# A recurrence feeding a routed expert layer on one core: outputs and evacuations first in the planner's queues, longer assumed waits

## The chip, the cores and the metric

The kernel runs on one core of a Trainium2 chip. The metric is device time of one execution in microseconds (us). The engines are TensorE (PE; its weight loads are shown as PEld), VectorE (DVE), ScalarE (ACT), GpSimd (POOL) and SyncE (SP, which only issues DMAs here).

## What is computed

Two layers follow one another. The first is a gated linear recurrence over the sequence, for 4 batches of 5056 steps and 256 channels; the second sends each of the 20224 rows to one of 8 experts, chosen by cosine similarity.

```python
sig = 1.0 / (1.0 + np.exp(-f_logit))
f = lower_bound + (1.0 - lower_bound) * sig
for t in range(S):
    h = f[:, t] * h + (1.0 - f[:, t]) * x[:, t]
    y[:, t] = h
x = y.reshape(B * S, D)                      # 20224 x 256
logits = xn @ en.T / tau                     # both normalised by row
expert_idx = np.argmax(logits, axis=1)
gate_w = softmax(logits)[rows, expert_idx]
for e in range(8):
    h = np.maximum(x[mask] @ w1[e], 0.0)     # 256 -> 1024
    out[mask] = gate_w[mask, None] * (h @ w2[e])   # 1024 -> 256
```

## The kernel before

**Recurrence.** The rows are cut into 40 chunks of 512 (the last has 256). For a chunk, `F_` and `X_` transpose the loaded gate logits and inputs on TensorE (lines 546 and 575), ScalarE makes the gate (554, 560), VectorE the product and the scan (583, 599). `Y_` transposes the result back (618) and ScalarE copies it into a row buffer (626). Two chunks are a group; `route_` computes logits, the best expert and each row's slot, and `gate_` the gate weight, which begins with a power function on POOL (775). `gate_` serves two groups at once (four chunks), except at the end, where it serves one group.

**Scratch.** Then POOL scatters these rows, 128 at a time, into a scratch tensor in HBM that is sorted by expert (line 832): 16 indirect DMAs for four chunks, which I call a set. A row carries its gate weight and its original row number.

**Experts.** `update_` counts rows for each expert and writes a table of complete tiles of 256 rows. It runs after the groups listed in line 1107; the last one covers all rows and fills the last tiles up with null rows. There are 86 tiles. `tile_` loads one with SyncE (996), and that load waits for every scratch scatter up to its update's group. TensorE transposes it (1013), VectorE copies that (1021), TensorE multiplies with the first weights in four steps (1036), ScalarE and VectorE take two each of the four results out of PSUM with a ReLU (1051, 1056), TensorE multiplies with the second weights (1067), ScalarE and VectorE evacuate one half each with the gate weight (1081, 1085), and POOL scatters the halves to their original rows (1091). There are 6 buffers of loaded tiles, 4 of outputs. For the first 70 tiles the first product has two PSUM banks and the second one, since the recurrence needs the others; after that four and two.

**Order.** Each engine works through a fixed list, in order, and waits for semaphores on the way. The lists come from a planner that runs when the program is built (`schedule`): it gives each operation an assumed cost, lets a dependent on another engine start `LAT` ns after its producer's end, and models a DMA as `DMA_FIX` ns behind a common bus of `DMA_RATE` bytes per ns. Where more than one operation of an engine is ready in the plan, the one with the lowest `prio` goes first. Recurrence, routing, gate and scratch scatters have the number of their chunk as `prio` (for a set, that of its last chunk). The operations of a tile have a number by these lines, in which `avail` lists the update that makes each tile complete; a tile's transposes and copy have 1.5 less:

```python
k = max(0, -(-(tok - E * (T - 1)) // T)) if u < len(ups) - 1 else NT
avail += [(u, g)] * (k - len(avail))
...
pr.prio = groups[g][-1] + 3.0 + 0.5 * (j - avail.index((u, g)))
```

Of the kernel before, what the change touches and what calls it, by code (L numbers as in the profile page):

```python
# [16 lines left out]
class Op:  # L17
    __slots__ = (
        "eng", "fn", "deps", "order", "dma", "val", "know", "used", "cost", "nbytes", "prio",
        "idx", "start", "end", "tag",  # L20
    )


class Prog:
# [2 lines left out]

    LAT = 90  # L30
    DMA_FIX = 1900
    DMA_RATE = 300.0

    def __init__(self):
        self.ops = []
# [55 lines left out]
    def schedule(self):  # L91
# [19 lines left out]
        while True:  # L111
# [22 lines left out]
            if o.dma is not None:  # L134
                bus = max(bus, free[e]) + o.nbytes / self.DMA_RATE
                o.end = max(bus, free[e]) + self.DMA_FIX
# [3 lines left out]
            for q, hard in succ[id(o)]:  # L140
                t = (o.end + self.LAT) if hard else free[e]
                if q.eng == e and o.dma is None and hard:
# [75 lines left out]
def bass_hgrn_recurrence__then__cosine_router_kernel(  # L218
# [22 lines left out]
    RW = 264  # L241
# [11 lines left out]
    pr = Prog()  # L253
    op = pr.op

    with ExitStack() as es:

        def sb(name, shape, dt=F32):
            return es.enter_context(nc.sbuf_tensor(name, shape, dt))
# [39 lines left out]
        Yt = [sb(f"Yt{q}", [P, 16, RW], BF16) for q in range(NY)]  # L299
# [28 lines left out]
        xsb = [sb(f"xsb{q}", [P, 2, RW], BF16) for q in range(NX)]  # L328
        ys = [sb(f"ys{q}", [P, DT, T], BF16) for q in range(2)]
        NHT = 2  # L330
        hT = [sb(f"hT{q}", [P, FT, T], BF16) for q in range(NHT)]
        NO = 4
        osb = [sb(f"osb{q}", [P, 2, D]) for q in range(NO)]
# [5 lines left out]
        def pool(fn, cost=400, **k):  # L339
            return op("pool", fn, cost, **k)  # L340

        def dve(fn, n, fast=False, **k):
            return op("dve", fn, 130 + n * (0.55 if fast else 1.04), **k)

        def act(fn, n, ptrs=0, **k):
            return op("act", fn, 190 + 0.833 * n + 93 * ptrs, **k)

        def pe(fn, cost, **k):
            return op("pe", fn, cost, **k)
# [42 lines left out]
        def iota(dst, pattern, base=0, mult=0, w=()):  # L392
# [10 lines left out]
            r=["ident"], w=["ident"],  # L403
# [19 lines left out]
            r=["scr"], w=["scr"],  # L423
# [8 lines left out]
        for q in range(R2):  # L432
            pool(lambda e, q=q: e.memset(exb[q][:], 1e-9), w=[("exb", q)])
        for q in range(NY):
            pool(lambda e, q=q: e.memset(Yt[q][:, :, 260:264], 0.0), w=[("ytz", q)])
        pool(lambda e: e.memset(oh[0][:, 64:72], 0.0), w=[("oh", 0)])

        def late_constants():
# [546 lines left out]


        evr = {}

        def tile_(j, u, g, phb, pob, ysb):

            qx, qy, qh, qo = j % NX, j % 2, j % NHT, j % NO
            last = u == len(ups) - 1

            def ld(e):
                r = e.value_load(tbl[u][j : j + 1, 0:1], min_val=0, max_val=NULLROW)
                return e.dma_start(
                    xsb[qx][:].bitcast(I32),
                    Xs[bass.ds(r, T), :].rearrange("(p s) r -> p s r", s=2),
                )

            rd = [("tbl", u), ("nt", 0), ("nt", 1)]
            rd += [("Xs", g_) for g_ in range(g + 1)]
            if last:
                rd += ["nul"]
            op("sp", ld, 700, r=rd, w=[("xsb", qx)], dma=f"xs{qx}", nbytes=135168)

            ysT = bank[ysb][:, 0:256].bitcast(BF16)

            def yt(e):
                o = ysT.rearrange("p (k s c) -> p k s c", k=2, s=2)  # L1010
                for s in range(2):
                    for kt in range(DT):
                        i = e.transpose(  # L1013
                            o[:, kt, s, :], xsb[qx][:, s, kt * P : (kt + 1) * P], identb[:]
                        )
                return i

            pr.prio -= YBOOST
            pe(yt, 310, r=[("xsb", qx), "identb"], x=[ysb])
            dve(  # L1020
                lambda e: e.tensor_copy(ys[qy][:].rearrange("p k c -> p (k c)"), ysT),  # L1021
                512, True, x=[ysb], w=[("ys", qy)],
            )
            pr.prio += YBOOST
            prev = None
            for m in range(4):
                pb = phb[m % len(phb)]

                def mm1(e, m=m, pb=pb):
                    if m == 0:  # L1030
                        evr[j] = e.value_load(
                            tbl[u][j : j + 1, 1:2], min_val=0, max_val=(E - 1) * WE
                        )
                    for fi in range(2):
                        for kt in range(DT):
                            i = e.matmul(  # L1036
                                bank[pb][:, fi * T : (fi + 1) * T],
                                wb[0][:, bass.ds(evr[j] + (kt * Fdim + (2 * m + fi) * P), P)],
                                ys[qy][:, kt, :],
                                start=(kt == 0), stop=(kt == DT - 1),  # L1040
                            )
                    return i

                prev = pe(
                    mm1, 490, r=[("ys", qy), ("tbl", u)] + [("w", i) for i in range(2 * E)],
                    x=[pb], order=[prev],
                )
                o = hT[qh][:, 2 * m : 2 * m + 2, :].rearrange("p f c -> p (f c)")
                if m % 2 == 0:
                    act(  # L1050
                        lambda e, o=o, pb=pb: e.activation(o, bank[pb][:], AF.Relu), 512,  # L1051
                        x=[pb], w=[("hT", qh, m)],
                    )
                else:
                    dve(
                        lambda e, o=o, pb=pb: e.tensor_scalar(  # L1056
                            o, bank[pb][:], 0.0, None, op0=ALU.max
                        ),
                        512, x=[pb], w=[("hT", qh, m)],
                    )  # L1060
            po = [bank[pob[0]][:, 0:D], bank[pob[1]][:, D : 2 * D]]
            one = pob[0] == pob[1]
            for m in range(4):
                def mm2(e, m=m):
                    for kf in (2 * m, 2 * m + 1):
                        for s in range(2):
                            i = e.matmul(  # L1067
                                po[s], hT[qh][:, kf, s * P : (s + 1) * P],
                                wb[1][:, bass.ds(evr[j] + kf * D, D)],
                                start=(kf == 0 and not (one and s)), stop=(kf == FT - 1),  # L1070
                                skip_group_check=one,
                            )
                    return i

                pe(
                    mm2, 480, r=[("hT", qh, m)] + [("w", i) for i in range(2 * E)],
                    x=sorted(set(pob)), order=[prev],
                )
            gx = [xsb[qx][:].bitcast(F32)[:, s, 128:129] for s in range(2)]
            act(  # L1080
                lambda e: e.activation(osb[qo][:, 0, :], po[0], AF.Copy, scale=gx[0]), 256, 1,  # L1081
                x=[pob[0]], r=[("xsb", qx)], w=[("osb", qo, 0)],
            )
            dve(
                lambda e: e.tensor_scalar(osb[qo][:, 1, :], po[1], gx[1], None, op0=ALU.mult),  # L1085
                340, x=[pob[1]], r=[("xsb", qx)], w=[("osb", qo, 1)],
            )
            for s in range(2):
                op(
                    "pool",  # L1090
                    lambda e, s=s: e.indirect_dma_start(  # L1091
                        out=out[:, :],
                        out_offset=bass.IndirectOffsetOnAxis(
                            ap=xsb[qx][:].bitcast(I32)[:, s, 129:130], axis=0
                        ),
                        in_=osb[qo][:, s, :],
                        in_offset=None,
                        bounds_check=N - 1,
                        oob_is_err=False,
                    ),  # L1100
                    1280, r=[("osb", qo, s), ("xsb", qx)], w=[("out", j, s)], dma=f"od{qo}_{s}",
                    nbytes=131072,
                )


# [11 lines left out]
        def put(j):  # L1117
            u, g = avail[j]
            pr.prio = groups[g][-1] + 3.0 + 0.5 * (j - avail.index((u, g)))
            if j < MERGED:  # L1120
                tile_(j, u, g, (5, 6), (7, 7), 5)
            else:
                tile_(j, u, g, (0, 1, 2, 6), (3, 7), 4)
# [22 lines left out]
        for j in range(NT):  # L1146
# [3 lines left out]
           r=["nul"])  # L1150
# [38 lines left out]
```

## Time and profile before

| | |
|---|---|
| runs, median (lowest, highest) | 775.52 us (771.86, 776.4), 3 runs |
| profiled execution | 781.91 us, of it span 780.0 us |
| mean granted TensorE clock | 0.881 of full speed |
| busy: PE, DVE, POOL, ACT | 76%, 51%, 50%, 44% of the span |
| scratch scatters (L832) on POOL | 158, 164.0 us |
| output scatters (L1091) on POOL | 172, 171.8 us |
| expert products (L1036, L1067) on PE | 217.1 and 186.1 us |

The profile is one execution; its rows are in time from the start of the span. Matmul rows overlap, and their ends are modelled. A row of POOL for an indirect DMA is the time in which POOL issues it, not the transfer. Expert work begins at 174 us, and the recurrence ends near 635 us; from there to 769 us there are only expert tiles.

### The profile page before, as it was taken

To read this page: it belongs to the slowest core of one execution; us is meant where nothing else is said; L and a number is where in the kernel's file an instruction comes from. 1 tells how busy PE (TensorE), PEld (TensorE's weight loads), DVE (VectorE), ACT (ScalarE), POOL (GpSimd) and SP (SyncE) were. 2 spreads that over 40 slices of the span, in tenths; PEclk is the share of its full clock that TensorE was granted. 3 is DMA by queue.
4 is the path that set the end of the run, shared out by engine and by line. 5 is a ranking of instruction groups with operands and counts; after the bars stand their busy time and mean duration, and the time that the engine had idled before them with its cause. 6 is when DMAs were issued, how large, how long until landed. Compare 5 with 4: busy or idle time off the path is not lost.

```text
span 780.0 us, 14923 instructions
## 1 busy us (share of the span) xinstructions
PE 591.7 (76%) x4656; PEld 430.5 (55%) x4656; DVE 399.0 (51%) x923; ACT 342.8 (44%) x574; POOL 387.7 (50%) x410
## 2 busy tenths in 40 slices
PE   5876676658868996879984698289848866999994
PEld 4543444436556764656763476167535544677773
DVE  4876556616435655354572465157705534445552
ACT  6976556534324623443542265064523522333431
POOL 4267757564644346563347335723572544335443
PEclk9998869769979999999997699579957977999997
DMA  9998886933313424332334244233311113223210
GB/s 277 284 276 209 223 168 195 222 119 106 100 59 104 153 69 134 98 111 84 121 109 136 72 151 127 80 129 123 106 60 56 63 42 117 83 84 99 65 58 1
DMA packets 80534, 95.04 MB, mean 122 GB/s; under 512 B 9089, under 2 KB 70797, under 8 KB 80464
## 3 DMA queue, kind: packets, MB, share of 16 engines
q1 hardware_dynamic: 56592, 54.15, 23.5%
q0 software_dynamic: 23872, 39.94, 18.5%
q8 instruction: 46, 0.75, 0.4%
q14 instruction: 24, 0.20, 0.1%
HBM read 69.83 MB, written 34.44 MB: 134 GB/s over the span
## 4 chain that ended last, share of the span: by engine, by line
PE 61%; another core or an unknown queue 11%; DVE 8%; issue 7%; ACT 7%; POOL 4%; DMA 1%; POOLq 0%; ACTq 0%; DVEq 0%
PE bank L1036 23%; PE bank L1067 19%; PE bank L618 4%; PE bank L546 4%; PE bank L575 3%; PE bank L666 3%; PE bank L1013 3%; POOL XsScratch L832 3%; DVE hb L599 2%; ACT hT L1051 2%; POOL nr L775 2%; DVE hT L1056 2%; DVE nx L583 1%; ACT th L554 1%
## 5 line engine op out<-in xcount | busy, mean ns | idle before, releaser
L1091 POOL DMA_INDIRECT out_dram<-osb,xsb x172 | 171.8, 999 | 257.8 <-DVE osb L1085 162.4
L1036 PE MATMUL bank<-ys,w1b 128*128 128x256 bf16 x1376 | 217.1, 290 | 57.3 <-issue 26.5
L1036 PEld LDWEIGHTS bank<-ys,w1b 128*128 x1376 | 135.5, 99 | 130.8 <-issue 92.0
L832 POOL DMA_INDIRECT XsScratch<-Yt,sli x158 | 164.0, 1038 | 82.9 <-issue 45.4
L1067 PE MATMUL bank<-w2b,hT 128*128 x1376 | 186.1, 282 | 21.2 <-DVE hT L1056 20.8
L1056 DVE TENSOR_SCALAR hT<-bank 128x512 bf16<-128x512 f32 x172 | 118.2, 687 | 90.7 <-PE bank L1036 54.7
L1067 PEld LDWEIGHTS bank<-w2b,hT 128*128 128x128 bf16 x1376 | 131.4, 101 | 43.6 <-issue 24.2
L1051 ACT ACTIVATE hT<-bank 128x512 bf16<-128x512 f32 x172 | 102.4, 596 | 114.5 <-PE bank L1036 87.9
L1081 ACT ACTIVATE osb<-bank,xsb 128x256 f32<-128x256 f32 x86 | 40.7, 473 | 174.2 <-PE bank L1067 104.9
L599 DVE TENSOR_TENSOR_SCAN hb<-fg,hb,nx 128x512 f32<-128x512 f32 (+4 forms) x78 | 97.1, 1245 | 1.4
L1085 DVE TENSOR_SCALAR osb<-bank,xsb 128x256 f32<-128x256 f32 x86 | 41.4, 482 | 103.5 <-ACT osb L1081 82.1
L618 PE MATMUL bank<-ident,hb 128*128 128x128 f32 x316 | 57.3, 311 | 33.4 <-issue 15.2
L546 PE MATMUL bank<-ident,fin 128*128 128x128 f32 x316 | 58.0, 314 | 23.8 <-ACT th L554 10.3
L618 PEld LDWEIGHTS bank<-ident,hb 128*128 128x128 f32 x316 | 40.4, 158 | 54.9 <-issue 33.2
L583 DVE SCALAR_TENSOR_TENSOR nx<-fg,bank 128x512 f32<-128x512 f32 (+1 forms) x80 | 53.9, 673 | 31.6 <-PE bank L575 8.5
L1021 DVE COPY ys<-bank 128x512 bf16<-128x512 bf16 x86 | 36.3, 422 | 64.5 <-issue 16.3
L626 ACT ACTIVATE Yt<-bank 128x512 bf16<-128x512 f32 x79 | 46.6, 590 | 47.9 <-remote 29.2
L560 ACT ACTIVATE fg<-th,cs 128x512 f32<-128x512 f32 (+1 forms) x80 | 64.6, 807 | 1.9
L575 PE MATMUL bank<-ident,xin 128*128 128x128 f32 x316 | 56.6, 308 | 8.9 <-DVE nx L583 8.0
L554 ACT ACTIVATE th<-bank 128x512 f32<-128x512 f32 (+1 forms) x80 | 47.1, 589 | 35.1 <-PE bank L546 20.6
L546 PEld LDWEIGHTS bank<-ident,fin 128*128 128x128 f32 x316 | 42.7, 162 | 28.7 <-ACT th L554 13.9
L611 ACT ACTIVATE sq<-hb 128x1024 f32<-128x1024 f32 (+1 forms) x40 | 41.6, 1041 | 22.4 <-DVE hb L599 21.7
(113 smaller groups left out, 419.7 us busy)
## 6 DMA issues: line engine op xcount, KB each, us to landing
fin<-in_f_logit_dram SPq DMA_DIRECT2D x39, 512.0 KB
xin<-in_x_dram SPq DMA_DIRECT2D x39, 512.0 KB
xsb<-XsScratch SPq DMA_DIRECT2D x86, 132.0 KB
w1b<-in_moe_w_dram POOLq DMA_DIRECT2D x8, 512.0 KB, 7.4
w2b<-in_moe_w_dram POOLq DMA_DIRECT2D x8, 512.0 KB, 7.7
out_dram<-osb,xsb POOLq DMA_INDIRECT x172
XsScratch<-Yt,sli POOLq DMA_INDIRECT x158
XsScratch<-nulr SPq DMA_DIRECT2D x8, 132.0 KB
```

Source lines behind the costliest of these rows:

```text
L546: i = e.transpose(bank[BF][:, b * P : (b + 1) * P], fin[q][:, b, dh * P : (dh + 1) * P], ident[:],)
L560: lambda e, dh=dh: e.activation(fg[c % 2][:, dh, 0:n], th[dh][:, 0:n], AF.Identity, bias=cs[:, dh, 0:1], scale=cs[:, dh, 1:2],),
L575: i = e.transpose(bank[BX][:, b * P : (b + 1) * P], xin[q][:, b, dh * P : (dh + 1) * P], ident[:],)
L583: lambda e, dh=dh: e.scalar_tensor_tensor(out=nx[c % 2][:, dh, 0:n], in0=fg[c % 2][:, dh, 0:n], scalar=1.0, in1=bank[BX][:, 0:n], op0=ALU. ...
L599: lambda e, dh=dh, s0=s0, s1=s1, init=init: e.tensor_tensor_scan(hb[c % NH][:, dh, s0:s1], fg[c % 2][:, dh, s0:s1], nx[c % 2][:, dh, s0:s1 ...
L618: i = e.transpose(bank[BY][:, (b % 2) * D + dh * P : (b % 2) * D + (dh + 1) * P], hb[c % NH][:, dh, b * P : (b + 1) * P], ident[:],)
L832: lambda e, j=o + j, i=o + k_ * 4 + b: e.indirect_dma_start(out=Xs[:, :], out_offset=bass.IndirectOffsetOnAxis(ap=sli[y][:, j : j + 1], axis=0
L1036: i = e.matmul(bank[pb][:, fi * T : (fi + 1) * T], wb[0][:, bass.ds(evr[j] + (kt * Fdim + (2 * m + fi) * P), P)], ys[qy][:, kt, :], start= ...
L1051: lambda e, o=o, pb=pb: e.activation(o, bank[pb][:], AF.Relu), 512,
L1056: lambda e, o=o, pb=pb: e.tensor_scalar(o, bank[pb][:], 0.0, None, op0=ALU.max),
L1067: i = e.matmul(po[s], hT[qh][:, kf, s * P : (s + 1) * P], wb[1][:, bass.ds(evr[j] + kf * D, D)], start=(kf == 0 and not (one and s)), stop ...
L1091: lambda e, s=s: e.indirect_dma_start(out=out[:, :], out_offset=bass.IndirectOffsetOnAxis(ap=xsb[qx][:].bitcast(I32)[:, s, 129:130], axis= ...
```

## The change

Two of the planner's constants, and the `prio` of three kinds of operations of `tile_`, become others. -1.0 is lower than any other `prio`. The number of instructions and their operands stay; the order of the lists may not.

```diff
-    LAT = 90
+    LAT = 300
     DMA_FIX = 1900
-    DMA_RATE = 300.0
+    DMA_RATE = 255.0
...
-            pool(lambda e, q=q: e.memset(Yt[q][:, :, 260:264], 0.0), w=[("ytz", q)])
+            pool(lambda e, q=q: e.memset(Yt[q][:, :, 260:RW], 0.0), w=[("ytz", q)])
...
+        EVP = lambda p: -1.0
+        OUTP = lambda p: -1.0
...
                     act(
                         lambda e, o=o, pb=pb: e.activation(o, bank[pb][:], AF.Relu), 512,
-                        x=[pb], w=[("hT", qh, m)],
+                        x=[pb], w=[("hT", qh, m)], prio=EVP(pr.prio),
                     )
...
-                        512, x=[pb], w=[("hT", qh, m)],
+                        512, x=[pb], w=[("hT", qh, m)], prio=EVP(pr.prio),
...
-                x=[pob[0]], r=[("xsb", qx)], w=[("osb", qo, 0)],
+                x=[pob[0]], r=[("xsb", qx)], w=[("osb", qo, 0)], prio=EVP(pr.prio),
...
-                340, x=[pob[1]], r=[("xsb", qx)], w=[("osb", qo, 1)],
+                340, x=[pob[1]], r=[("xsb", qx)], w=[("osb", qo, 1)], prio=EVP(pr.prio),
...
                     1280, r=[("osb", qo, s), ("xsb", qx)], w=[("out", j, s)], dma=f"od{qo}_{s}",
-                    nbytes=131072,
+                    nbytes=131072, prio=OUTP(pr.prio),
```

Two unused fields are added to the class `Op`.

## Rows read from the trace of the kernel before

**Rows 1.** The page: busy time, share of the span and instructions of each engine.

```profile
PE 591.7 (76%) x4656; PEld 430.5 (55%) x4656; DVE 399.0 (51%) x923; ACT 342.8 (44%) x574; POOL 387.7 (50%) x410
```

**Rows 2.** Windows: stretch, length, busy us (instructions) by engine, clock, DMA share, GB/s.

```profile
186.70:241.60 54.90, 40.64 (x318) 29.46 (x318) 22.03 (x53) 15.52 (x27) 29.62 (x30) 0.88 0.26 80
291.70:346.50 54.80, 39.90 (x332) 30.00 (x330) 27.50 (x58) 21.12 (x37) 33.21 (x32) 1.00 0.38 119
411.00:436.50 25.50, 10.50 (x65) 7.62 (x63) 4.65 (x14) 5.21 (x8) 17.47 (x18) 0.67 0.32 107
483.30:508.40 25.10, 8.11 (x49) 5.75 (x47) 5.35 (x19) 3.02 (x5) 17.97 (x18) 0.59 0.33 100
561.00:586.00 25.00, 11.70 (x65) 8.44 (x64) 4.36 (x15) 5.33 (x8) 17.56 (x18) 0.61 0.23 75
616.00:628.80 12.80, 5.57 (x50) 3.85 (x46) 3.37 (x14) 1.77 (x4) 10.14 (x11) 0.83 0.15 51
350.00:404.00 54.00, 51.14 (x439) 37.09 (x440) 29.73 (x55) 25.48 (x44) 18.73 (x20) 0.99 0.36 111
440.00:476.00 36.00, 34.73 (x299) 26.12 (x298) 22.41 (x42) 21.71 (x37) 11.93 (x13) 0.95 0.47 144
510.00:554.00 44.00, 42.19 (x358) 31.76 (x358) 28.42 (x51) 26.35 (x44) 12.67 (x13) 0.94 0.41 130
```

**Rows 3.** The chain that ended last, tail: start, us, what (two successive tiles).

```profile
734.67 2.24 PE bank L1036 x16
...
738.98 2.21 PE bank L1036 x16
```

**Rows 4.** Timeline of POOL, first, last and what follows of an unbroken set: start, us, instruction.

```profile
410.91 0.96 POOL L832 DMA_INDIRECT XsScratch<-Yt,sli  x1 [0.30 <-DVE val L912]
...
430.11 0.96 POOL L832 DMA_INDIRECT XsScratch<-Yt,sli  x1 [0.30 <-issue]
431.37 1.00 POOL L1091 DMA_INDIRECT out_dram<-osb,xsb  x1 [0.30 <-issue]
...
440.32 0.98 POOL L1091 DMA_INDIRECT out_dram<-osb,xsb  x1 [6.67 <-DVE osb L1085]
```

**Rows 5.** Timeline of TensorE inside that set.

```profile
421.69 0.40 PE L1013 MATMUL bank<-identb,xsb 128*128 128x128 bf16 x4 [2.89 <-ACT hT L1051]
```

**Rows 6.** Timeline of VectorE inside that set.

```profile
435.10 0.42 DVE L1021 COPY ys<-bank 128x512 bf16<-128x512 bf16 x1 [14.82 <-issue]
```

**Rows 7.** Timeline of POOL, a mixed set: its first rows and its last scatter.

```profile
291.67 0.97 POOL L832 DMA_INDIRECT XsScratch<-Yt,sli  x1 [0.31 <-issue]
294.64 0.99 POOL L1091 DMA_INDIRECT out_dram<-osb,xsb  x1 [2.00 <-DVE osb L1085]
...
345.50 0.96 POOL L832 DMA_INDIRECT XsScratch<-Yt,sli  x1 [0.31 <-issue]
```

**Rows 8.** Waits of all engines: who waited for whom, us in total, times, longest.

```profile
POOL out_dram L1091 <- DVE osb L1085: 162.4, 53, 11.2
```

**Rows 9.** Groups by line: busy us, mean ns of one, idle before.

```profile
L1056 DVE TENSOR_SCALAR hT<-bank 128x512 bf16<-128x512 f32 x172 | 118.2, 687 | 90.7 <-PE bank L1036 54.7 <-remote 20.1 <-PE bank L618 9.1
...
L599 DVE TENSOR_TENSOR_SCAN hb<-fg,hb,nx 128x512 f32<-128x512 f32 (+4 forms) x78 | 97.1, 1245 | 1.4
```

**Rows 10.** The chain around the first unbroken set: two handovers between engines.

```profile
407.54 0.02 issue
...
410.22 0.13 issue
```

**Rows 11.** DMA issues by line: size and median us from issue to landing.

```profile
XsScratch<-nulr POOLq DMA_DIRECT2D x2, 66.0 KB, 6.2
```

**Rows 12.** Windows: one cycle, from one gate's power function to the next.

```profile
404.60:476.90 72.30, 53.11 (x426) 39.20 (x425) 35.27 (x88) 32.56 (x55) 34.45 (x35) 0.83 0.37 118
```

**Rows 13.** Windows: output scatters alone (L1091), in the mixed set and that cycle.

```profile
291.70:346.50 54.80, 16.59 (x16) 1.00 0.38 119
404.60:476.90 72.30, 15.75 (x16) 0.83 0.37 118
```

More of the change, by code (lines that the diff above doesn't have):

```diff
@@ L19 @@
         "eng", "fn", "deps", "order", "dma", "val", "know", "used", "cost", "nbytes", "prio",
-        "idx", "start", "end", "tag",
+        "idx", "start", "end", "tag", "astart", "aend",
     )
 class Prog:
-    LAT = 90
+    LAT = 300
     DMA_FIX = 1900
-    DMA_RATE = 300.0
+    DMA_RATE = 255.0
     def __init__(self):
```

## The prediction, made before the changed kernel ran

> **What bounds the kernel now.** I began with the busy line of the page [rows 1]: TensorE is busy 591.7 of 780.0 us, every other engine about half, so what counts is where TensorE stands idle. A window table over chosen stretches then shows where. In three stretches without scatters to the scratch it is busy 51.14 of 54.00, 34.73 of 36.00 and 42.19 of 44.00 us: 5.94 of 134 us idle, 4.4% (its last three rows) [rows 2]. In two stretches that hold a set of 16 scratch scatters with output scatters among them (I call these mixed) it is idle 14.3 and 14.9 us of 55. In the three that hold 16 scratch scatters in an unbroken row it is idle 15.0, 17.0 and 13.3 us of only 25, at a mean granted clock of 0.67, 0.59 and 0.61 of full speed, so partly at the lower level, 1.2 GHz. When the recurrence is over and only expert tiles are left, a tile takes 738.98 - 734.67 = 4.31 us, all of it TensorE [rows 3]. No order of queues shortens that; what can be won are the idle times further up.
>
> The timeline of POOL shows what the two kinds of set look like. In an unbroken one, 16 scatters run from 410.91 to 431.07, one each 1.28 us, and only then the next pair of output scatters; the pair after that waits 6.67 us for VectorE [rows 4]. Inside that row TensorE's transposes of a loaded tile start at 421.69 and by the model of their ends are over at 422.09 [rows 5], yet the VectorE copy of their result, which needs nothing else that is late, starts at 435.10 [rows 6]. So in an unbroken row the word that TensorE has finished comes up to 13 us late, and it comes only once POOL has stopped. In a mixed set POOL itself waits between the scatters for outputs [rows 7], and those pauses let the news through. This is a reading of coincidence in time; the trace does not show what connects POOL with TensorE. By the Trainium skill, "Perfetto Trace Analysis", section "Tensor Engine Instruction (MATMUL, LD_WEIGHTS)", a matmul's reported end is an estimate; the trace agrees so far as a dependent starting 13 us behind it shows.
>
> **What a set costs, mixed and unbroken.** Mixed: 14.6 us idle on average, less 4.4% of 55 us that is idle anyway (2.4), is 12.2; the clock adds at most 0.12 x 40.6 = 4.9 in the first and nothing in the second, on average 2.4, so 14.6 us. Unbroken: 15.1 idle, less 1.1, is 14.0; its 10.1 us of busy time at a mean of 0.62 lose 3.8; the stretch after it still runs at 0.95, about 2 us more [rows 2]. Together 19.8 us. The difference is 5.2 us for a set.
>
> **The change part by part.** Output scatters at priority -1. Before, a set has the number of its last chunk as priority (27, 31, 35 in the three unbroken cases), and the tiles then in flight have a half more or above, by line 1119; so the planner put the set first. In the mixed sets the tiles had lower numbers. Now outputs always go first, so the three unbroken sets become mixed as long as outputs are there. How long is that? A set must be complete before the tiles of the next update can be loaded. By lines 1107 to 1112, 41 tiles are available without the set of chunk 27, and POOL's outputs up to tile 35 stand ahead of it: five tiles are left. A mixed set spends about two scratch scatters between two pairs of outputs (16 in 54.8 us, with 16 outputs, so 6.85 us a pair) [rows 2, 7, 13]. Five pairs cover 10 of the 16; six stay in a row. Price of the new set: 10/16 x 14.6 = 9.1, and for six in a row three quarters of the row of eight at 616 us, which is idle 7.2 us and loses 0.9 to the clock [rows 2]: 6.1. Together 15.2 against 19.8: 4.6 us won a set, 14 us for three. The last, smaller sets (8, 4 and 2 scatters) have few outputs left; I put them at 3 us, by the row of eight: 8.1 us, of which the same share of a quarter is 2, and 1 for the others. The lower bound of the whole is 0 (news comes late in mixed sets as well), the upper bound all that the three unbroken rows cost over a stretch without scatters, 3 x 19.8 = 59 us.
>
> What the scatter is moved past: on POOL, the scratch scatters and the power function of the next gate wait behind two outputs, 2 x 1.3 us, or for longer when the planner thought the output ready and it is not: POOL waits 162.4 us for the VectorE half of an output already [rows 8]. Behind the scratch scatters stand SyncE's loads of tiles, behind these the transposes on TensorE. In the other direction the tile buffers, read by the output scatter, come free sooner, and so SyncE's loads start sooner.
>
> Expert evacuations at priority -1 on ScalarE and VectorE. Nothing is added; where both are ready an evacuation of 0.69 us (VectorE) now goes ahead of, say, a scan of 1.25 us rather than behind it [rows 9]. Outside the sets 4.4% of TensorE's time is idle, in the whole 596 us after the first expert tile some 400 are outside: 18 us at stake. Half of that is the most that I credit to the edit, 9 us, and the same is the bound of a loss, when the recurrence comes late and leaves TensorE less to fill with. I take 3, since an expert tile of this stretch has only two banks for its first product.
>
> The longer assumed wait, 300 for 90 ns, and 255 for 300 bytes per ns, change the planned order alone. Actual handovers between engines are 0.02 to 0.13 us [rows 10], so the longer figure is the less true; it makes the planner put other work between producer and consumer. The trace of before does not show what order comes out. Its bounds are the same 18 us, half of it either way; I take 0. Unused fields and a memset whose end is written as RW, equal to 264, cost nothing: the instructions are the same.
>
> The sum is 14 + 3 + 3 = 20 us. The profiled execution takes 781.9 us, 780.0 of it span, so it would take about 762; the median of the runs is 775.5, 6 us below it, and gives **756 us**.
>
> **The rivals.** First, and on the other side: the outputs starve the tiles. POOL works through its list in order, so it holds back scratch scatters while it waits for an output [rows 8], and a set that took 20 us now takes five pairs x 6.85 = 34 us and six scatters x 1.28 = 8 us; the five tiles are used up at 34. A 66 KB transfer from POOL's queue lands after 6.2 us [rows 11]; with as much again for the load, as an estimate, TensorE has no expert tile for 8 + 6 + 6 = 20 us. A cycle has TensorE busy 53.1 us [rows 12] for 8 tiles [rows 13], so about 18.6 us of recurrence, which could fill all of it or, where it has run already, nothing. Half filled, three sets lose 30 and win 17: 788 us. It decides where the filling is under some 14 us a set. Against it speaks that the planner sees the gap and moves the recurrence there; for it, that it sees neither the late news nor the lower clock. By the Trainium skill, "TensorE: Matmul & The Clock Gate", Part 1, "Architectural detail", the queue of GpSimd is strict first in, first out; the rows agree, since nothing else of POOL's runs in the 162.4 us in which it waits for outputs [rows 8].
>
> Second, no change: the late news is tied to the number of scatters and not to their row. The mixed sets cost 14.6 against 19.8, and with 6 still in a row the gain could be eaten by the reordering: 770 to 781.
>
> Third, a larger gain: short pauses are enough to clear the news, so that two thirds of 59 us go, and the evacuations bring their 9: 775.5 - 48 = 728. The mixed sets, still idle for 14 us, speak against it.
>
> That the change does not do what it says is possible for the evacuations: a priority only acts where two are ready at once, and both engines are half idle. This would leave 759.
>
> **How the numbers follow.** Forecast (745 to 768) 0.50; larger gain 0.13; no change 0.18; starvation 0.19. A measurement of this kernel, whose runs spread 4.5 us, can tell 1%, 7.8 us, from no change. Faster takes the first two and a little less at their edge, 0.62; same 0.19; slower 0.19. The range runs from 730, where about a third of the larger gain is left out, to 787, which leaves out the worse half of starvation.
>
> **What would show it.** POOL's timeline: no row of 16 scratch scatters after 400 us, output pairs inside each set, six or so scatters left at its end. Windows over each of the three sets: TensorE idle under 15 us in place of 15 plus the lower clock; the granted clock of these stretches over 0.8. No VectorE copy 13 us behind its transposes. The stretches without sets stay near 95% busy. Wrong would be: sets still unbroken, or mixed with the same stalls; or TensorE idle before the first tile of an update with SyncE's load the last to arrive, which is starvation.

## The result, and the profile after

The median goes from 773.75 us (4 runs, 771.86 to 776.4) to 754.16 us (4 runs, 746.88 to 763.02), and the ratio is 0.9713 [0.9632, 0.9794]. The forecast was 756. The ratio leaves out the slowest of the four runs after, 763.02 us, which was over 1.5% above the fastest; the two medians as they stand give 0.975. That run is also the profiled execution of the changed kernel, and the profiled execution of before (781.91) lies above its four runs too; the two profiles are 18.9 us apart, the medians 19.6.

The busy line of the page after, beside [rows 1]: every engine has the work it had.

```profile
PE 589.0 (77%) x4656; PEld 436.1 (57%) x4656; DVE 397.6 (52%) x923; ACT 343.6 (45%) x574; POOL 391.3 (51%) x410
```

I divided both spans at the first output scatter and at the last scratch scatter. The first stretch is the start, the second has recurrence and experts together, the third only experts. In a window row, length less the first busy figure is TensorE's idle time. Before:

```profile
0.00:182.80 182.80, 122.10 (x860) 83.22 (x861) 108.52 (x255) 112.29 (x171) 106.47 (x131) 0.83 0.85 216
182.80:656.50 473.70, 363.96 (x2933) 267.44 (x2932) 237.27 (x573) 190.26 (x331) 229.42 (x228) 0.88 0.32 99
656.50:772.10 115.60, 105.66 (x869) 79.86 (x866) 53.17 (x96) 40.28 (x73) 50.88 (x52) 0.98 0.24 73
```

After:

```profile
0.00:200.80 200.80, 129.62 (x851) 88.55 (x852) 109.12 (x256) 113.11 (x170) 104.15 (x132) 0.79 0.77 194
200.80:572.70 371.90, 295.02 (x2441) 223.39 (x2440) 203.44 (x516) 166.93 (x291) 210.31 (x200) 0.92 0.37 114
572.70:751.10 178.40, 164.35 (x1369) 124.11 (x1366) 85.06 (x152) 63.62 (x115) 75.86 (x79) 1.00 0.24 76
```

Idle time: the start 60.7 to 71.2 us (10.5 lost), the middle 109.7 to 76.9 (32.8 won), the end 9.9 to 14.1 (4.1 lost). Busy time falls by 2.7, the stretch behind the last output grows by 2.2; together 18.7 of the 18.8 us between the spans. The middle also ends earlier: 47 tiles have been scattered out when the last scratch scatter goes, where it was 60. The recurrence runs ahead of the experts. Since 13 tiles have thus moved from the middle to the end, the two are best read together: their idle time falls from 119.7 to 90.9 us, 28.7 won, more than forecast, and over a third of it is lost at the start.

The order of POOL's indirect DMAs from about 400 us on, read off the two timelines (x is a scratch scatter, O an output scatter; first before, then after):

```
...xxxxxxxxxxxxxxxxOOOOOOOOOOOOOOOOxxxxxxxxxxxxxxxxOOOOOOOOOOOOOOOOxxxxxxxxxxxxxxxxOOOOOOOOOOxxxxxxxxOOxxxx...
...xxxxOOxxxOOxxxxOOxxxxOOxOOOOOOOOxxxOOxxOxOxxOOxxxxOOxxxOOxOOxxxOOxxxxOOxOOOOxxOOxxxOO...
```

No unbroken set is left: the longest row has four. Where [rows 4] had a scatter each 1.28 us for 20 us, the timeline of POOL after shows waits for outputs between them (start, us, instruction, and in brackets the wait):

```profile
339.27 0.96 POOL L832 DMA_INDIRECT XsScratch<-Yt,sli  x1 [0.30 <-issue]
340.54 0.96 POOL L832 DMA_INDIRECT XsScratch<-Yt,sli  x1 [0.30 <-issue]
341.80 0.95 POOL L832 DMA_INDIRECT XsScratch<-Yt,sli  x1 [0.30 <-issue]
345.04 0.98 POOL L1093 DMA_INDIRECT out_dram<-osb,xsb  x1 [2.28 <-DVE osb L1087]
...
360.18 0.98 POOL L1093 DMA_INDIRECT out_dram<-osb,xsb  x1 [2.52 <-ACT hT L1053]
...
380.65 0.99 POOL L1093 DMA_INDIRECT out_dram<-osb,xsb  x1 [6.00 <-DVE osb L1087]
```

Windows over the five sets of 16 after, beside the three unbroken ones of [rows 2]:

```profile
203.40:241.00 37.60, 25.89 (x205) 19.43 (x203) 16.39 (x38) 13.27 (x23) 24.56 (x24) 0.90 0.37 115
274.50:317.30 42.80, 30.47 (x260) 23.66 (x259) 23.02 (x54) 20.03 (x34) 25.61 (x24) 0.96 0.43 131
339.30:384.00 44.70, 32.57 (x267) 25.02 (x265) 23.38 (x59) 17.62 (x30) 26.18 (x26) 0.89 0.41 129
409.10:448.00 38.90, 30.03 (x237) 23.41 (x235) 18.88 (x46) 18.12 (x30) 26.17 (x24) 0.87 0.47 148
476.70:521.00 44.30, 34.94 (x268) 23.90 (x267) 22.27 (x58) 18.03 (x32) 26.70 (x27) 0.88 0.23 72
```

Idle: 11.7, 12.3, 12.1, 8.9 and 9.4 us, at a granted clock of 0.87 to 0.96, where the unbroken sets had 13 to 17 us at 0.59 to 0.67. News is still late, but by less. The worst pair of transposes and copy within these sets, from the timelines of TensorE and of VectorE:

```profile
491.72 0.39 PE L1015 MATMUL bank<-identb,xsb 128*128 128x128 bf16 x4
...
496.16 0.42 DVE L1023 COPY ys<-bank 128x512 bf16<-128x512 bf16 x1 [3.93 <-remote]
```

That is 496.16 - 492.11 = 4.05 us, beside 13 us in [rows 5, 6]. The table of waits answers to [rows 8], where POOL waited 162.4 us for this half of an output:

```profile
POOL out_dram L1093 <- DVE osb L1087: 113.7, 40, 7.6
```

### The profile page after: what moved, and what is told of

It reads as the page before. It is cut to its first block, busy times and chain, and to the rows that moved or that the text cites. A ratio compares the mean times of both kernels' runs of the same rounds, so it can differ in the third digit from the quotient of the medians.

```text
span 761.2 us, 14962 instructions
## 1 busy us (share of the span) xinstructions
PE 589.0 (77%) x4656; PEld 436.1 (57%) x4656; DVE 397.6 (52%) x923; ACT 343.6 (45%) x574; POOL 391.3 (51%) x410
## 4 chain that ended last, share of the span: by engine, by line
PE 54%; issue 7%; ACT 5%; DVE 5%; another core or an unknown queue 5%; POOL 3%; DMA 0%; POOLq 0%; DVEq 0%; ACTq 0%
PE bank L1038 22%; PE bank L1069 18%; ACT hT L1053 3%; PE bank L618 3%; PE bank L546 3%; PE bank L1015 3%; PE bank L575 3%; POOL nr L775 2%; PE bank L666 2%; POOL out_dram L1093 1%; DVE hT L1058 1%; ACT osb L1083 1%; PE bank L688 1%; DVE osb L1087 1%
## 5 line engine op out<-in xcount | busy, mean ns | idle before, releaser
L1038 PE MATMUL bank<-ys,w1b 128*128 128x256 bf16 x1376 | 209.8, 287 | 57.2 <-ACT hT L1053 18.5
L618 PE MATMUL bank<-ident,hb 128*128 128x128 f32 x316 | 57.7, 312 | 24.1 <-ACT Yt L626 10.3
L575 PE MATMUL bank<-ident,xin 128*128 128x128 f32 x316 | 59.9, 322 | 6.5 <-DVE nx L583 5.7
L1015 PE MATMUL bank<-identb,xsb 128*128 128x128 bf16 x344 | 35.1, 228 | 20.7 <-ACT hT L1053 16.0
```

The lines of the kernel that those rows point to most:

```text
L575: i = e.transpose(bank[BX][:, b * P : (b + 1) * P], xin[q][:, b, dh * P : (dh + 1) * P], ident[:],)
L618: i = e.transpose(bank[BY][:, (b % 2) * D + dh * P : (b % 2) * D + (dh + 1) * P], hb[c % NH][:, dh, b * P : (b + 1) * P], ident[:],)
L1015: i = e.transpose(o[:, kt, s, :], xsb[qx][:, s, kt * P : (kt + 1) * P], identb[:])
L1038: i = e.matmul(bank[pb][:, fi * T : (fi + 1) * T], wb[0][:, bass.ds(evr[j] + (kt * Fdim + (2 * m + fi) * P), P)], ys[qy][:, kt, :], start= ...
```

## The experiments

The first four ran on a chip where the kernel before takes 779.69 us (7 runs). The other eight came to three further chips, on which it takes 640.31, 641.03 and 639.78 us. That was not foreseen, and divides the evidence in two. Which chip gave the result above, where the kernel before takes 773.75 us, is not known.

### Which edit mixes the sets

Priorities alone (both constants as before):

```diff
-    LAT = 300
+    LAT = 90
-    DMA_RATE = 255.0
+    DMA_RATE = 300.0
```

> Evacuations and outputs at priority -1, but waits of 90 ns and 300 bytes per ns as before. The planned lists differ from those before in 134 of 407 places on GpSimd; the sets of chunks 27, 31 and 35 become mixed, but the recurrence still ends as late (the last set's scatter stands behind 62 tiles' outputs, before behind 60). Theory A, the prediction's (unbroken sets are the cost, mixing them is the gain): ratio to the kernel before 0.97 to 0.985. Theory B (the gain comes from the longer assumed wait, which makes the planner run the recurrence ahead of the tiles): ratio 0.99 to 1.01.

Measured: 765.62 us, 0.9804 [0.9761, 0.9847], by the ratio 15.3 us won. POOL's row of scatters is mixed up to the last set (longest row five, then the eight), and the recurrence does not run ahead: its last scratch scatter comes behind 62 tiles.

The assumed wait alone:

```diff
-    DMA_RATE = 255.0
+    DMA_RATE = 300.0
-        EVP = lambda p: -1.0
-        OUTP = lambda p: -1.0
+        EVP = lambda p: p
+        OUTP = lambda p: p
```

> The assumed wait of 300 ns alone; priorities and the bus rate as before. In the lists all sets are mixed already and the last set stands behind 46 tiles' outputs. Theory A: the sets are mixed, so ratio 0.97 to 0.985 as well, for another reason than predicted. Theory B: ratio 0.965 to 0.985, as the whole change. A third theory (the bus rate does it, through the start): ratio 0.99 to 1.01.

Measured: 740.57 us, 0.9470 [0.9402, 0.9539]. With no priority at all the sets are mixed, and the gain is larger than that of the whole change. The three stretches of its windows, divided as above:

```profile
0.00:172.90 172.90, 118.40 (x862) 80.33 (x863) 107.60 (x256) 110.99 (x171) 109.13 (x132) 0.86 0.90 226
172.90:542.70 369.80, 290.92 (x2386) 221.49 (x2385) 198.99 (x511) 164.85 (x286) 208.84 (x198) 0.91 0.37 114
542.70:727.20 184.50, 171.66 (x1414) 127.88 (x1412) 87.54 (x157) 65.25 (x118) 77.79 (x81) 1.00 0.25 75
```

The middle is that of the changed kernel (78.9 us idle, 76.9 there; 46 tiles out, 47 there). The start is not: 54.5 us idle, 71.2 there.

The bus rate alone:

```diff
-    LAT = 300
+    LAT = 90
-        EVP = lambda p: -1.0
-        OUTP = lambda p: -1.0
+        EVP = lambda p: p
+        OUTP = lambda p: p
```

> The bus rate of 255 alone. The lists keep the sets of 31 and 35 unbroken, seven and nine scatters in a row in the two sets before, and the recurrence ends at tile 60. Theories A and B: ratio 0.99 to 1.015. Third theory (rate): 0.97 to 0.98.

Measured: 809.93 us, 1.0363 [1.0287, 1.0439]. Three unbroken sets remain (chunks 27, 31 and 35); the first output comes at 197.9 us, and the three stretches are idle for 76.5, 122.7 and 9.4 us. The later start of the changed kernel goes with the rate: 197.9 and 200.8 us with it, 172.9 with the wait alone, 182.8 before. The profiled execution of the priorities alone, the longest of its five runs, has 192.4 without it, so the size is uncertain here. On the three chips below, the first output comes at 172.8 to 173.9 us in the traces with the rate of 255 and at 163.9 to 165.3 in those with 300, 8 to 10 us earlier.

The changed kernel without its priorities, on a chip where the kernel before takes 641.03 us:

```diff
-        EVP = lambda p: -1.0
-        OUTP = lambda p: -1.0
+        EVP = lambda p: p
+        OUTP = lambda p: p
```

> The changed kernel without its priorities (300 ns and 255 bytes per ns kept): GpSimd's and SyncE's lists are those of the changed kernel to the last place, TensorE's differ in 28 places of 1085, VectorE's in 32. Theory B (the wait does it): on a chip where the kernel before takes some 775 us the ratio of the whole change, 0.96 to 0.98; on a chip where it takes 640 us and no news is late, only the lists' other merits count: less idle in the mixed stage, a later start and 22 lone tiles on two banks, 0.99 to 1.02. Theory A as predicted (the priorities do it): 0.99 to 1.01 on either.

Measured: 644.19 us, 1.0047 [1.0031, 1.0063], which is the unaltered change's 1.0031 [1.0013, 1.0049] (below, on another chip) within the intervals. The instruction lists say why: between these two kernels POOL's and SP's are the same, and VectorE's differ in 32 places, TensorE's in 28 and ScalarE's in 2, where before and after differ in 273, 103, 782, 825 and 455. With the output priority alone taken out, no list differs at all. That the priorities add nothing to the change where news is late follows from these lists; it was not run there.

### Whether unbroken sets are what costs

The changed kernel with all scratch scatters put ahead of the outputs:

```diff
-                            w=[("Xs", g)], dma=f"sc{y}", nbytes=67584, chain=False,
+                            w=[("Xs", g)], dma=f"sc{y}", nbytes=67584, chain=False, prio=-2.0,
```

> The changed kernel, but with the scratch scatters at priority -2, ahead of the outputs: all five sets after the first expert tile become unbroken rows of 16, while the recurrence still runs ahead (last set at tile 46). Theory A: each unbroken set costs 4 to 8 us more than a mixed one, so 20 to 40 us above the changed kernel, ratio to before 0.995 to 1.025. Theory B in its pure form: as the changed kernel, ratio 0.965 to 0.98.

Measured: 798.63 us, 1.0235 [1.0183, 1.0288]. All five sets are unbroken again, while the recurrence stays as far ahead (46 tiles out). Its first stretch is like the changed kernel's (75.1 us idle), its middle is idle for 111.5 in place of 76.9. Three of its sets and one stretch between them:

```profile
281.00:305.00 24.00, 9.71 (x66) 7.15 (x63) 4.58 (x21) 3.71 (x7) 17.34 (x18) 0.69 0.28 85
361.00:385.00 24.00, 6.42 (x42) 4.27 (x39) 4.60 (x10) 1.67 (x3) 17.05 (x18) 0.66 0.29 90
434.00:458.00 24.00, 9.77 (x61) 7.10 (x60) 4.51 (x21) 3.52 (x6) 16.96 (x18) 0.63 0.26 84
...
305.00:353.00 48.00, 43.85 (x388) 34.72 (x389) 32.05 (x58) 28.34 (x49) 15.58 (x17) 0.94 0.43 130
```

Inside the first of them, from the timelines of POOL, TensorE and VectorE, first and last scatter, transposes and their copy:

```profile
281.27 0.96 POOL L832 DMA_INDIRECT XsScratch<-Yt,sli  x1 [2.73 <-DVE Yt L809]
...
300.23 0.96 POOL L832 DMA_INDIRECT XsScratch<-Yt,sli  x1 [0.30 <-issue]
...
287.68 0.40 PE L1015 MATMUL bank<-identb,xsb 128*128 128x128 bf16 x4 [2.41 <-issue]
...
298.41 0.42 DVE L1023 COPY ys<-bank 128x512 bf16<-128x512 bf16 x1 [7.48 <-remote]
```

The copy starts 10.3 us behind its transposes' end, late as in [rows 5, 6]. It starts before the row's last scatter, though, and so does a ScalarE copy inside the unbroken set of [rows 4] of the kernel before. That copy's transposes on TensorE were over at 418.79, and two scatters of the row were still to come:

```profile
417.73 1.06 PE L618 MATMUL bank<-ident,hb 128*128 128x128 f32 x4
...
428.10 0.60 ACT L626 ACTIVATE Yt<-bank 128x512 bf16<-128x512 f32 x1 [5.52 <-remote]
```

So the prediction's "only once POOL has stopped" goes too far: the news is late in a row, but some of it comes before the row's end. The two ratios stand 1.0235 / 0.9713 = 1.054 apart, with both intervals taken together [1.043, 1.064]; on 754 us that is about 40 us, 8 for a set (the two ratios come from different sessions, each against the kernel before in its own). Order alone brings the cost back, with the same instructions.

The same two kernels where the kernel before takes 639.78 us, first the change, unaltered, then this edit again:

> The changed kernel unaltered. Where the kernel before takes 640 us: 1.00 to 1.01, as without its priorities (1.0047). Where it takes some 775 us: 0.965 to 0.98 again.

> The changed kernel with the scratch scatters ahead of the outputs, so with unbroken sets. Where the kernel before takes 640 us and no news is late, theory A expects that unbroken rows cost little: within 1.5% of the changed kernel in this call (it was 5.4% above it where news is late). If unbroken sets cost by holding up outputs and their buffers alone, on any chip: 4 to 6% above the changed kernel here too.

Measured: 641.79 us, 1.0031 [1.0013, 1.0049], and 647.94 us, 1.0100 [1.0053, 1.0147]. The change wins nothing there, and unbroken sets cost 1.0100 / 1.0031, 0.7% (4.4 us by the ratios, 6.2 by the medians, about 1 for a set). In the trace of the second, TensorE is idle for only 0.4 to 0.8 us in each of the five unbroken sets; the first two:

```profile
175.50:198.00 22.50, 22.14 (x203) 17.83 (x202) 16.10 (x38) 13.42 (x24) 17.62 (x17) 1.00 0.42 131
227.00:248.50 21.50, 21.07 (x190) 16.82 (x190) 17.64 (x44) 14.28 (x25) 16.62 (x17) 1.00 0.54 160
```

### Whether it is the rows of scatters by themselves

The kernel before with 21 more scatters of 66 KB where only experts run, in three rows of seven behind tiles 66, 73 and 80 (they write to a tensor that nothing reads):

```diff
+            for _ in range(7 if j in (66, 73, 80) else 0):
+                d = len(dumps)
+                oo = op(
+                    "pool",
+                    lambda e, d=d: e.indirect_dma_start(
...
+                    1280, r=["nulr", "didx"], w=[("dump", d)], dma="dump", nbytes=67584,
+                    order=[oo], prio=-5.0,
```

> The kernel before with 21 more scatters of 66 KB of zero rows into a scratch tensor that nothing reads, in three rows of 7 behind the outputs of tiles 66, 73 and 80, where only expert tiles run and TensorE is never idle. A row takes GpSimd 9 us; four output buffers cover 17 us. Theory A: 5 to 8 us of TensorE's time for each row, 15 to 24 us in all, ratio 1.02 to 1.035. Theory C: nothing beyond the spread form of the same 21 scatters.

And the same 21, one behind each tile from 64 to 84 (`1 if 64 <= j < 85 else 0`):

> The same 21 scatters, one behind the outputs of each of the tiles 64 to 84. GpSimd then needs 3.8 us of the 4.3 us of a tile. Theory A: 0 to 4 us, ratio 1.00 to 1.006. Theory C: as much as the rows.

Measured, where the kernel before takes 640.31 us: 641.16 us, 1.0017 [0.9995, 1.0038] in rows, 642.23 us, 1.0028 [1.0009, 1.0048] spread out. Neither costs TensorE anything to speak of, and 15 to 24 us were expected of the rows. But the runs fell on a chip where no news is late, so they do not test the rows where it is. The trace of the first also holds the three unbroken sets of the kernel before, and they are harmless on this chip (the last row is a stretch without a set):

```profile
351.30:376.00 24.70, 23.39 (x212) 17.82 (x210) 17.15 (x42) 15.40 (x26) 19.17 (x19) 1.00 0.44 139
402.60:427.00 24.40, 23.54 (x216) 17.80 (x216) 19.29 (x47) 15.91 (x27) 19.41 (x17) 1.00 0.51 158
456.60:480.00 23.40, 22.70 (x206) 17.26 (x204) 16.23 (x40) 13.85 (x24) 18.22 (x18) 1.00 0.21 68
...
300.00:350.00 50.00, 47.95 (x425) 36.38 (x425) 30.97 (x71) 25.57 (x46) 21.52 (x20) 1.00 0.38 118
```

TensorE is idle for 1.3, 0.9 and 0.7 us in them, at a clock of 1.00, where [rows 2] had 15.0, 17.0 and 13.3 at about 0.6: the same list, the same 16 scatters. The timeline in the first one shows the same handover:

```profile
355.60 0.39 PE L1017 MATMUL bank<-identb,xsb 128*128 128x128 bf16 x4
...
356.03 0.42 DVE L1025 COPY ys<-bank 128x512 bf16<-128x512 bf16 x1 [0.38 <-PE bank L1017]
```

The copy follows 0.04 us behind the transposes, in the middle of a row. By the Trainium skill, "Perfetto Trace Analysis", section "Tensor Engine Instruction (MATMUL, LD_WEIGHTS)", a matmul's end in a trace is estimated; this row shows the estimate near the truth, so it does not make up the 10 to 13 us seen where news is late.

### Whether a pause lets the news through

The kernel before, with a power function of 2.9 us on POOL behind every fourth scatter of the three unbroken sets:

```diff
+                        if groups[gg[0]][0] >= 24 and len(gg) > 1 and nsc and nsc % 4 == 0:
+                            gap = pool(
+                                lambda e: e.tensor_tensor(dum[:], half[:], half[:], ALU.pow),
+                                2900, r=["half"], w=["dum"], order=[gap],
+                            )
```

> The kernel before, its order kept, with a power function of 2.9 us on GpSimd (its result is not used) after every fourth scatter of the sets of chunks 27, 31 and 35. GpSimd stays busy and the sets end 9 us later, but no more than four scatters are issued without a pause. Theory A (a row of scatters holds up the news of TensorE's progress, a pause lets it through): each set costs TensorE less, ratio to before 0.97 to 0.99. Theory C (the cost goes by the number of scatters, or by GpSimd being busy, or by the wait for the set's end): ratio 1.00 to 1.03.

> The kernel with pauses in three sets once more. Where the kernel before takes some 775 us, theory A (a row of scatters without a pause holds up the news): 0.97 to 0.99; theory C (scatters or a busy GpSimd by number): 1.02 to 1.04, as on the chip without late news. Where it takes 640 us: 1.03 again.

Measured: 658.85 us, 1.0292 [1.0240, 1.0344], and 659.96 us, 1.0293 [1.0255, 1.0332]. Both fell on chips where no news is late, so there was nothing to let through, and they show only that nine pauses of 2.9 us, 26 us of POOL's time, and a somewhat different order cost 19 us. (The order was not quite kept: 14 and 18 outputs stand between the three sets, where it was 16 and 16.) The question stays open.

### A version without the rate, with the banks moved

The assumed wait alone, and four banks for the first product from tile 46 on, since the recurrence now ends there:

```diff
-    LAT = 90
+    LAT = 300
...
-        MERGED = 70
+        MERGED = 46
```

> The assumed wait of 300 ns alone, and the tiles from 46 on (70 before) on four PSUM banks for the first product and two for the second, since the recurrence now ends there. With two banks a lone tile takes 4.75 us in the trace, with four 4.15. 24 tiles by 0.6 us are 14 us less than with the wait alone (0.947): ratio to before 0.925 to 0.935. If the ends of tiles are held by outputs and not by banks: 0.945 to 0.95.

Measured, where the kernel before takes 640.31 us: 629.39 us, 0.9824 [0.9780, 0.9867]. The ratio was forecast for a chip with late news and missed, but by its ratio it is the fastest version there, ahead of both kernels. In the changed kernel's own end, the chain shows what the banks do. A lone tile with two banks has ScalarE on the chain (start, us, what; one tile to the next, then two tiles with four banks):

```profile
594.41 0.60 ACT hT L1053
595.02 0.13 issue
595.15 1.25 PE bank L1038 x8
...
599.22 0.60 ACT hT L1053
...
719.70 1.99 PE bank L1038 x16
...
723.76 2.20 PE bank L1038 x16
```

4.81 us against 4.06. In this version the same place in the order has no ScalarE:

```profile
522.41 2.18 PE bank L1038 x16
524.59 1.41 PE bank L1069 x12
...
526.72 2.18 PE bank L1038 x16
```

A tile takes 4.31 us, and the end stretch is idle for 5.9 us; in the unaltered change, on the chip where it takes 641.79 us, it is 9.3. What the rate and the banks bring singly was not separated, nor was this version run where news is late.

## Why the prediction was right, and where it was not

**Right: where the time is.** On the chip where news is late, unbroken sets cost about what the prediction read from [rows 2], and mixing them is what wins: order alone brings back 40 us. The difference between an unbroken and a mixed set was estimated at 5.2 us (19.8 and 14.6), and 4.6 with six scatters left in a row; the mixed sets are idle for 11 us on average, and a set made unbroken again costs 8. The granted clock in them is over 0.8, as foreseen. The size, 756 for 754, is partly luck, as the next points show.

**Wrong: which edit mixes them.** The sum had 14 + 3 us from the output priority and 0 from the wait and the rate. In the whole change the output priority does nothing: without it every list is the same. The step that failed is the term of the longer assumed wait ("I take 0"): it asked what the new order would do to stretches without sets, and not whether it would move the sets. Alone, the wait mixes all of them and takes 5.3% off the time. The code has the reason, argued from the plan's costs: a tile's chain through one of its two banks costs 2935 ns and six handovers, 3475 ns at 90 and 4735 at 300, while TensorE's own work for a tile is put at 4190. At 90 TensorE is the plan's bound, at 300 the chain is, and the two are equal at 209. The plan then gives the free slots to the recurrence, which runs ahead by 13 tiles; tiles in flight then have lower numbers than the set's chunk, and their outputs go first by the old rule. The planner's lists, worked out from the code of the kernel before with other waits and not run on the chip, agree: from 60 to 150 ns two or three sets stay unbroken, and the last scratch scatter stands behind 60 tiles; from 211 ns on no set does, and that scatter stands behind 51 tiles at 240 and 46 at 300. Alone, at 90, the priorities do what the prediction said of them: 15.3 us [11.9, 18.6] where the sum had 20 with the evacuations.

**Wrong: the rate.** Also taken at 0, it costs 3.6% alone, and inside the change the later start: the first output at 200.8 us for 172.9, with 16.7 us more idle. The wait alone gains 5.3% where the whole change, in another session, gains 2.9%. The rows show the loads of the start at 194 GB/s in place of 226; how the order of the lists makes that was not followed.

**Wrong in detail.** No six scatters are left in a row. With the recurrence ahead there is no lack of tiles, so starvation did not come either, and the last small sets are mixed as well. The evacuation priority, 3 us in the sum, shows nothing in the whole change (1.0047 and 1.0031 without and with it); at the wait of 90 it was not run apart from the output priority. The end pays for the new order: 39 lone tiles in place of 26, and of these the 23 from 47 to 69 have two banks, where it was 10; 13 more at 0.5 to 0.75 us are 6 to 10 us, an estimate from the tile times above (4.81 us with two banks, 4.06 and 4.31 with four).

**Right with a limit.** That news is late in unbroken rows was called a coincidence in time. It is confirmed on the chip where order alone was changed. It does not hold on two others, whose traces show unbroken rows with TensorE hardly idle; on one of these the change is worth -0.3%. On the third, unbroken rows were run only with pauses in them, and there TensorE's clock stays at 1.00 too. So the gain is the avoidance of something that not every chip shows. What makes the news late where it is late, and whether pauses by themselves let it through, stays open.

## What to carry to other kernels

A planner's latency is not a small correction: it decides which resource the plan holds for the bound, and with that which stage runs ahead. Before an edit is credited, compare the instruction lists with and without it; of the four parts of this change that act on the planner, one made the gain, one took a good part of it back, and two did next to nothing beside it. Where a stage's end moves in the order, move what was tied to it (here the tile at which PSUM banks change hands), and try the kernel on more than one chip, since 2.9% on one was nothing on another.

## What the runs showed of the hardware

The same program, with the same lists, takes 774 us where the result was measured, 780 on the chip of the first four experiments, and 640 on three others. Where it takes 774 or 780 us, VectorE starts up to 13 us behind the reported end of TensorE's matmuls while POOL issues indirect scatters in a row. On one chip where it takes 640 us the same handover takes 0.04 us, and TensorE stays at a granted clock of 1.00 (2.4 GHz) in rows where it had 0.6. In the rows of 16 without pauses POOL issues a scatter every 1.26 to 1.33 us in the traces of the first kind and every 1.32 to 1.41 in those of the second, so the chips of 640 us do not issue them faster.
